# Summing the first two key/value chunks inside TensorE, and moving the first score ahead of the other query turns

## The chip, the cores and the metric

The kernel runs on one core of a Trainium2 chip. The metric is device time in microseconds (us) of one execution. Before the change it was 1057.65 us (median of 3 runs, 1057.03 to 1057.91).

A ratio below is the mean time of one kernel's fast runs over that of the kernel before in the same rounds on the same chip, so it is not quite the ratio of the medians quoted beside it.

## The reference, cut to what matters

```python
kv_pool = kv.reshape(B, H//4, 4, W//4, 4, C).mean(axis=(2, 4))   # B=4, H=384, W=32, C=128
k = v = kv_pool.reshape(B, -1, C) @ w_sr                         # 768 keys = 6 chunks of 128
a = softmax(q @ k.T / sqrt(C))                                   # 12288 queries in each batch
x = a @ v
out = (relu(x @ w_gate) * (x @ w_val)) @ w_out                   # d_ff = 1536
```

Each of the 768 keys of a batch is a mean over 4 lines (`dh`) by 4 columns (`dw`) of the key/value image, projected by `w_sr`. Nothing can be scored before a chunk of 128 keys is pooled, turned (transposed), projected and written.

## The kernel before

Batch 0 has an opening of its own, in which nothing else is there to do. The key/value image comes in three pairs of chunks, each pair in four transfers, one for each line:

```python
def kv_load(b, pair):
    parts = work.tile([128, r, 2, r, C], FP32, tag="kv_in", bufs=3)
    ...
    for dh in range(r):
        nc.sync.dma_start(parts[:, dh]..., rows[dh])       # 512 KB each
    for h in range(2):
        kv_in[b, 2 * pair + h] = parts[:, :, h]
```

VectorE adds the four lines in three instructions of 128x512; TensorE adds the four columns, as four turns that accumulate in one PSUM bank:

```python
def add_lines(eng, b, jc, i):     # i=0: lines 0+1, i=1: lines 2+3, i=2: the two sums
    ...
def turn_pooled(b, jc, pooled):
    tp = bank([128, 128])
    for i in range(n):            # n = 4 columns
        nc.tensor.matmul(tp, pooled[:, i, :], ident, is_transpose=True,
                         start=(i == 0), stop=(i == n - 1))
    kv_Ts[b, jc] = work.tile([128, 128], FP32, tag="kvT", name="kvT")
    nc.vector.tensor_copy(kv_Ts[b, jc], tp)
def project(b, jc): ...           # TensorE: w_sr times the turned chunk
def keep_keys(b, jc): ...         # VectorE: PSUM to kv16, the key write
```

The opening, cut:

```python
keep_warm(34); q_cast(0); q_turn_pe(0); keep_warm(34)      # idle matmuls
...
add_lines(nc.vector, 0, 0, 0); add_lines(nc.vector, 0, 1, 0)
add_lines(nc.vector, 0, 0, 1); add_lines(nc.vector, 0, 0, 2)
turn_pooled(0, 0, ...); add_lines(nc.vector, 0, 1, 1)
project(0, 0); keep_keys(0, 0)
for i in range(1, GRP):
    q_turn_pe(i)
    if i == 1: add_lines(nc.vector, 0, 1, 2)
for jc in range(NJC):
    scores(0, jc); turn_values(0, jc, nc.scalar.copy)
    turn_pooled(0, jc + 1, ...)
    for k in range(1, GRP): scores(k, jc)
    project(0, jc + 1)
    ...                                                     # adds of the chunks after
    keep_keys(0, jc + 1)
    ...                                                     # more adds; value products; weight loads
```

`scores` is a TensorE matmul of 128x512 and an exponential on ScalarE, for four query tiles `k`. After the six chunks the first FFN projection starts (`value_proj`), and from there TensorE is full to the end.

The softmax here doesn't subtract the row's maximum and nothing guards it: scores larger than these inputs give would overflow.

Of the kernel before, what the change touches and what calls it, by code (L numbers as in the profile page):

```python
# [9 lines left out]
FP32 = mybir.dt.float32  # L10
FP16 = mybir.dt.float16
# [5 lines left out]
def kernel(  # L17
# [22 lines left out]
    nc = tc.nc  # L40

    B, N, C = q.shape
    _, H, W, _ = kv.shape
    r = 4
    J = (H // r) * (W // r)
    NJC = J // 128
    HC = H // NJC
    D_FF = moe_w_gate.shape[1]
    NFB = D_FF // 128
    T = 512  # L50
    NS = T // 128
    NST = N // T
    NT = B * NST
    GRP = 4
# [8 lines left out]
    work = ctx.enter_context(tc.tile_pool(name="work", bufs=2))  # L63
    psum = ctx.enter_context(tc.tile_pool(name="psum", bufs=8, space=bass.MemoryType.PSUM))

    def bank(shape, dtype=FP32):
        return psum.tile(shape, dtype, tag="bank", name="bank_ps")


    q16s, qTs, q32s = {}, {}, {}  # L70

    def q_load(g):
        if not 0 <= g < NG:
            return
        b, n0 = divmod(g * GRP * T, N)
        q16 = work.tile([128, GRP * NS, C], FP16, tag="q16", bufs=2)
        nc.gpsimd.dma_start(  # L77
            q16, q[b, n0 : n0 + GRP * T, :].rearrange("(p s) c -> p s c", p=128)
        )
        q16s[g] = q16  # L80

    def q_turn(g):
        if not 0 <= g < NG:
            return
        q16 = q16s.pop(g)
        qT = work.tile([128, GRP * NS, 128], FP16, tag="qT", bufs=3)
        nc.sync.dma_start_transpose(qT, q16.rearrange("p s c -> p (s c)"))
        qTs[g] = qT
# [7 lines left out]
            q32s[i] = q32[:, i - i0]  # L96

    def q_cast(i):
        q16 = work.tile([128, NS, C], FP16, tag="q16s", bufs=2, name="q16s")
        nc.scalar.copy(q16, q32s[i])  # L100
        q16s[0, i] = q16

    def q_turn_pe(i):
        q16 = q16s.pop((0, i))
        qt_ps = bank([128, NS, 128], FP16)
        for s in range(NS):
            nc.tensor.transpose(qt_ps[:, s, :], q16[:, s, :], ident16)
        if i == 0:
            qTs[0] = work.tile([128, GRP * NS, 128], FP16, tag="qT", bufs=3, name="qT")
        nc.vector.tensor_copy(qTs[0][:, i * NS : (i + 1) * NS, :], qt_ps)  # L110

    def qT_of(k):
        s0 = (k % GRP) * NS
        return qTs[k // GRP][:, s0 : s0 + NS, :].rearrange("c s p -> c (s p)")
# [4 lines left out]
    kv_in = {}  # L119
# [11 lines left out]
    s2s, s1s, kv_Ts, key_banks = {}, {}, {}, {}  # L131

    def add_lines(eng, b, jc, i):
        if i == 0:
            s2s[b, jc] = work.tile([128, 2, r, C], FP32, tag="kv_s2", bufs=2, name="kv_s2")
        parts, s2 = kv_in[b, jc], s2s[b, jc]
        if i < 2:
            eng.tensor_tensor(s2[:, i], parts[:, 2 * i], parts[:, 2 * i + 1], op=ALU.add)  # L138
        else:
            s1s[b, jc] = work.tile([128, r, C], FP32, tag="kv_s1", bufs=2, name="kv_s1")  # L140
            eng.tensor_tensor(s1s[b, jc], s2[:, 0], s2[:, 1], op=ALU.add)  # L141
            del kv_in[b, jc], s2s[b, jc]
# [8 lines left out]
    def turn_pooled(b, jc, pooled):  # L151
        tp = bank([128, 128])
        n = pooled.shape[1]
        for i in range(n):
            nc.tensor.matmul(  # L155
                tp, pooled[:, i, :], ident, is_transpose=True,
                start=(i == 0), stop=(i == n - 1),
            )
        kv_Ts[b, jc] = work.tile([128, 128], FP32, tag="kvT", name="kvT")
        nc.vector.tensor_copy(kv_Ts[b, jc], tp)  # L160

    def project(b, jc):
        key_banks[b, jc] = bank([128, 128])
        nc.tensor.matmul(key_banks[b, jc], w_sr_f32, kv_Ts.pop((b, jc)), start=True, stop=True)  # L164

    def keep_keys(b, jc):
        nc.vector.tensor_scalar(  # L167
            kv16[:, b, jc, 0:C], key_banks.pop((b, jc)), 1.0 / (r * r), None, op0=ALU.mult
        )

    def turn_values(b, jc, copy):
        vt = bank([128, 128], FP16)
        nc.tensor.transpose(vt, kv16[:, b, jc, 0:C], ident16)  # L173
        copy(kv16[:, b, jc, C : 2 * C], vt)
# [5 lines left out]
    def scores(k, jc):  # L180
        if jc == 0:
            aTs[k] = work.tile([128, NJC, T], FP16, tag="aT", bufs=4, name="aT")
        s_ps = bank([128, T])
        nc.tensor.matmul(s_ps, kv16[:, k // NST, jc, 0:C], qT_of(k), start=True, stop=True)  # L184
        nc.scalar.activation(aTs[k][:, jc, :], s_ps, AF.Exp, scale=qk_scale)  # L185

    def values(k, jc, half):
        if jc == 0:
            x_banks[k, half] = bank([128, 2, C + 1])
            if half == 0:  # L190
                x16s[k] = work.tile([128, NS, C], FP16, tag="x16", bufs=3, name="x16")
                rinvs[k] = work.tile([128, NS], FP32, tag="rinv", bufs=3, name="rinv")
        x_ps = x_banks[k, half]
        for i in range(2):
            s = 2 * half + i
            nc.tensor.matmul(  # L196
                x_ps[:, i, :], aTs[k][:, jc, s * 128 : (s + 1) * 128],
                kv16[:, k // NST, jc, C : 2 * C + 1],
                start=(jc == 0 and i == 0), stop=(jc == NJC - 1), skip_group_check=True,
            )  # L200
# [80 lines left out]
    ident = const.tile([128, 128], FP32)  # L281
    make_identity(nc, ident)
    ident16 = const.tile([128, 128], FP16)
# [11 lines left out]
    wg16 = const.tile([128, D_FF], FP16)  # L295
    wv16 = const.tile([128, D_FF], FP16)
    wo16 = const.tile([128, NFB, 128], FP16)

    def pool_of(jc):
        return nc.gpsimd if jc == NJC - 2 else nc.vector  # L300


    idle = bank([128, 128])

    def keep_warm(n):
        for _ in range(n):
            nc.tensor.matmul(idle, ident16, ident16, start=True, stop=True)

    keep_warm(34)
    q_cast(0)  # L310
    q_turn_pe(0)
    keep_warm(34)
    for i in range(1, GRP):
        q_cast(i)
    add_lines(nc.vector, 0, 0, 0)
    add_lines(nc.vector, 0, 1, 0)
    add_lines(nc.vector, 0, 0, 1)
    add_lines(nc.vector, 0, 0, 2)
    turn_pooled(0, 0, s1s.pop((0, 0)))
    add_lines(nc.vector, 0, 1, 1)  # L320
    project(0, 0)
    keep_keys(0, 0)
    for i in range(1, GRP):
        q_turn_pe(i)
        if i == 1:
            add_lines(nc.vector, 0, 1, 2)
    for jc in range(NJC):
        scores(0, jc)
        turn_values(0, jc, nc.scalar.copy)
        ahead = jc + 1 < NJC  # L330
        if ahead:
            turn_pooled(0, jc + 1, s1s.pop((0, jc + 1)))
        for k in range(1, GRP):
            scores(k, jc)
        if ahead:
            project(0, jc + 1)
        if ahead and jc % 2 == 1:
            add_lines(nc.vector, 0, jc + 2, 1)
        if ahead:
            keep_keys(0, jc + 1)  # L340
        if jc % 2 == 1 and ahead:
            add_lines(nc.vector, 0, jc + 2, 2)
        elif jc + 3 < NJC:
            add_lines(pool_of(jc + 2), 0, jc + 2, 0)
            add_lines(nc.vector, 0, jc + 3, 0)
            add_lines(nc.vector, 0, jc + 2, 1)
            add_lines(nc.vector, 0, jc + 2, 2)
        if jc > 0:
            for k in range(2):
                for half in range(2):  # L350
                    values(k, jc - 1, half)
        if jc == 2:
            for own in (slice(0, D_FF // 2), slice(D_FF // 2, D_FF)):
                nc.gpsimd.dma_start(wv16[:, own], moe_w_val[:, own])
                nc.gpsimd.dma_start(wg16[:, own], moe_w_gate[:, own])
            q_load(1)
            q_turn(1)
            nc.gpsimd.dma_start(wo16, moe_w_out.rearrange("(fb f) c -> f fb c", f=128))
            q_load(2)
    for half in range(2):  # L360
        values(0, NJC - 1, half)
        keep_values(0, half)
# [12 lines left out]
    for k in range(LAG, last + 1):  # L375
# [4 lines left out]
        b = k // NST + 1  # L380
        at = k % NST - (NST - NJC - 6)
        for step in range(NFB):
            kO, kF = k - LAG - 1, k - LAG
            half, i = divmod(step // 2, NJC // 2)
# [4 lines left out]
            if k == LAG:  # L389
                own, left = left[:2], left[2:]  # L390
# [69 lines left out]
```

## Time and profile before

| what | value | how to read it |
|---|---|---|
| time | 1057.65 us | median of 3 runs |
| span in the profile | 1055.9 us | first to last instruction |
| first FFN projection | 38.05 us | the end of the opening |
| from there to the end | 1017.9 us | TensorE full |
| key writes of chunks 0 to 5 start at | 14.71, 18.92, 24.72, 27.30, 31.27, 33.84 us | the pace of the opening |
| clock at half | to 4.40, 11.23 to 18.05 and 21.47 to 24.88 us | the trace's clock records; before the first one, the matmul spacing |

The opening is 3.6% of the time.

### The profile page before, as it was taken

How to read it: one execution, taken by the hardware profiler on the slowest of the kernel's cores; microseconds unless marked ns; L12 is line 12 of the kernel's file. 1: busy time of each engine (PE TensorE's matmuls, PEld its weight loads, DVE VectorE, ACT ScalarE, POOL GpSimd, SP SyncE). 2: the span in 40 equal slices, each digit the busy share in tenths (PEclk: the TensorE clock that was granted, in tenths of full speed). 3: DMA queues.
4: the chain of work that ended last, by engine and by line, in shares of the span. 5: the costliest groups of instructions: out<-in, count | busy, mean ns of one | idle time of the engine just before them, and what ended most of it. 6: DMA issues, size and time to landing. Idle time of an engine off the chain costs nothing.

```text
span 1055.9 us, 26244 instructions
## 1 busy us (share of the span) xinstructions
PE 1035.0 (98%) x9998; PEld 691.4 (65%) x9998; DVE 926.2 (88%) x1809; ACT 912.2 (86%) x1758; POOL 107.1 (10%) x127
## 2 busy tenths in 40 slices
PE   6999999999999999999999999999999999999997
PEld 4566666666666666666666666666666666666664
DVE  4788889999898989898989898999888888888896
ACT  3898888888888888888888888888888888888886
POOL 2000044200000005500000003340000000000000
PEclk8999999999999999999999999999999999999999
DMA  8732365431322435523224144542331322212111
GB/s 292 125 81 52 66 195 160 72 71 46 71 67 51 86 114 144 149 66 72 56 61 86 32 86 130 149 132 56 77 79 37 82 55 64 54 45 53 46 32 46
DMA packets 125710, 90.76 MB, mean 86 GB/s; under 512 B 103312, under 2 KB 103952, under 8 KB 125584
## 3 DMA queue, kind: packets, MB, share of 16 engines
q1 hardware_dynamic: 120144, 75.85, 26.9%
q0 software_dynamic: 5440, 13.24, 7.6%
q8 instruction: 78, 1.28, 0.5%
q14 instruction: 48, 0.39, 0.1%
HBM read 52.76 MB, written 25.17 MB: 74 GB/s over the span
## 4 chain that ended last, share of the span: by engine, by line
PE 96%; DVE 1%; ACT 1%; DMA 1%; issue 0%; SPq 0%; ACTq 0%; DVEq 0%
PE bank_ps L254 24%; PE bank_ps L240 24%; PE bank_ps L229 23%; PE bank_ps L196 12%; PE bank_ps L184 12%; DMA parts<-in_kv_dram 1%; PE bank_ps L155 1%; PE bank_ps L164 1%; DVE hT L243 0%; ACT aT L185 0%; DVE kv_s L138 0%; DVE kv_s L141 0%; SPq L127 0%; ACT o_sb L264 0%; PE bank_ps L173 0%
## 5 line engine op out<-in xcount | busy, mean ns | idle before, releaser
L243 DVE SCALAR_TENSOR_TENSOR hT<-bank_ps,val 128x512 f16<-128x512 f32 x1152 | 764.2, 686 | 99.7 <-ACT val L233 70.6
L233 ACT CAST val<-bank_ps 128x512 f16<-128x512 f32 x1152 | 677.7, 590 | 118.7 <-PE bank_ps L229 115.8
L254 PEld LDWEIGHTS <-hT 128*128 128x128 f16 x4608 | 351.1, 98 | 207.2 <-issue 3.0
L254 PE MATMUL bank_ps<-wo,hT 128*128 128x128 f16 x4608 | 443.4, 219 | 2.1 <-DVE hT L243 2.0
L240 PE MATMUL bank_ps<-xT,wg 128*128 128x512 f16 x1152 | 435.7, 378 | 1.6 <-DVE hT L243 1.5
L229 PE MATMUL bank_ps<-xT,wv 128*128 128x512 f16 x1152 | 436.6, 379 | 0.4 <-ACT x L205 0.4
L185 ACT ACTIVATE aT<-bank_ps 128x512 f16<-128x512 f32 x576 | 345.8, 604 | 7.6 <-PE bank_ps L184 7.6
L196 PE MATMUL bank_ps<-kv,aT 128*128 128x129 f16 x2304 | 223.6, 220 | 0.0
L196 PEld LDWEIGHTS <-aT 128*128 128x128 f16 x2304 | 177.5, 98 | 67.9 <-issue 0.4
L184 PE MATMUL bank_ps<-qT,kv 128*128 128x512 f16 x576 | 217.7, 381 | 0.5 <-DVE kv L167 0.4
L240 PEld LDWEIGHTS <-wg 128*128 128x128 f16 x1152 | 111.5, 97 | 65.4
L229 PEld LDWEIGHTS <-wv 128*128 128x128 f16 x1152 | 112.7, 98 | 0.6 <-issue 0.5
L205 DVE CAST x<-bank_ps 128x256 f16<-128x256 f32 x186 | 76.9, 414 | 2.1 <-PE bank_ps L196 2.1
L77 POOL DMA_DIRECT2D q<-in_q_dram x23 | 12.5, 543 | 552.6 <-DMA qT<-q 552.4
L138 POOL TENSOR_TENSOR kv_s<-parts 128x512 f32<-128x512 f32 x37 | 46.5, 1269 | 167.7 <-DMA parts<-in_kv_dram 145.0
L266 DVE TENSOR_TENSOR o_sb<-bank_ps,inv 128x512 f32<-128x512 f32 x93 | 63.2, 680 | 0.0
L184 PEld LDWEIGHTS <-kv 128*128 128x128 f16 x576 | 56.6, 98 | 2.3 <-issue 0.8
L206 DVE RECIPROCAL rinv<-bank_ps 128x2 f32<-128x2 f32 x192 | 30.5, 159 | 1.0 <-ACT x L205 0.7
L141 POOL TENSOR_TENSOR kv_s<-kv_s 128x512 f32<-128x512 f32 x18 | 22.8, 1268 | 1.4
L210 DVE TENSOR_TENSOR inv<-rinv 128x4 f32<-128x4 f32 x96 | 19.7, 205 | 3.3
L155 PE MATMUL bank_ps<-ident,kv_s 128*128 128x128 f32 x24 | 5.2, 353 | 8.7 <-DVE kv_s L141 8.4
L146 POOL TENSOR_TENSOR s<-kv_s 128x256 f32<-128x256 f32 x18 | 13.1, 726 | 1.4
(39 smaller groups left out, 108.6 us busy)
## 6 DMA issues: line engine op xcount, KB each, us to landing
parts<-in_kv_dram SPq DMA_DIRECT2D x48, 512.0 KB, 6.4
out_dram<-o_sb SPq DMA_DIRECT2D x96, 256.0 KB, 2.2
q<-in_q_dram POOLq DMA_DIRECT2D x23, 512.0 KB, 5.1
xT<-x SPq DMA_TRANSPOSE x94, 2.5
q<-in_q_dram SPq DMA_DIRECT2D x1, 768.0 KB, 8.3
wv<-in_moe_w_val_dram POOLq DMA_DIRECT2D x2, 192.0 KB, 4.6
wg<-in_moe_w_gate_dram POOLq DMA_DIRECT2D x2, 192.0 KB, 5.0
wo<-in_moe_w_out_dram POOLq DMA_DIRECT2D x1, 384.0 KB, 10.0
```

What stands on the lines that cost most here:

```text
L138: eng.tensor_tensor(s2[:, i], parts[:, 2 * i], parts[:, 2 * i + 1], op=ALU.add)
L184: nc.tensor.matmul(s_ps, kv16[:, k // NST, jc, 0:C], qT_of(k), start=True, stop=True)
L185: nc.scalar.activation(aTs[k][:, jc, :], s_ps, AF.Exp, scale=qk_scale)
L196: nc.tensor.matmul(x_ps[:, i, :], aTs[k][:, jc, s * 128 : (s + 1) * 128], kv16[:, k // NST, jc, C : 2 * C + 1], start=(jc == 0 and i == 0) ...
L205: copy(x16s[k][:, own, :], x_ps[:, :, 0:C])
L206: nc.vector.reciprocal(rinvs[k][:, own], x_ps[:, :, C])
L229: nc.tensor.matmul(va_ps, wv16[:, fb * 128 : (fb + 1) * 128], xTs[k], start=True, stop=True)
L233: nc.scalar.copy(val, va_ps)
L240: nc.tensor.matmul(g_ps, wg16[:, fb * 128 : (fb + 1) * 128], xTs[k], start=True, stop=True)
L243: nc.vector.scalar_tensor_tensor(hTs[k][:, fb, :], g_ps, 0.0, vals.pop((k, fb)), op0=ALU.max, op1=ALU.mult)
L254: nc.tensor.matmul(o_ps[:, s, :], hTs[k][:, fb, s * 128 : (s + 1) * 128], wo16[:, fb, :], start=(fb == 0 and s == 0), stop=(fb == NFB - 1) ...
L266: nc.vector.tensor_tensor(o_sb, o_ps, inv2.to_broadcast([128, NS, 128]), op=ALU.mult)
```

## The change

Its intent: VectorE's six adds for chunks 0 and 1 go; instead TensorE turns each of the four lines as it lands, sixteen accumulating turns for a chunk. The first score no longer waits for the query turns of the other tiles, the cast of queries and the turned chunk get a third buffer, and the adds of later chunks move to other places.

```diff
-        q16 = work.tile([128, NS, C], FP16, tag="q16s", bufs=2, name="q16s")
+        q16 = work.tile([128, NS, C], FP16, tag="q16s", bufs=3, name="q16s")
...
+    def turn_lines(b, pair):
+        tps = [bank([128, 128]) for _ in range(2)]
+        for dh in range(r):
+            for h in range(2):
+                for dw in range(r):
+                    nc.tensor.matmul(
+                        tps[h], kv_in[b, 2 * pair + h][:, dh, dw, :], ident, is_transpose=True,
+                        start=(dh == dw == 0), stop=(dh == dw == r - 1),
+                    )
...
-    keep_warm(34)
     for i in range(1, GRP):
         q_cast(i)
-    add_lines(nc.vector, 0, 0, 0)
...
-    project(0, 0)
-    keep_keys(0, 0)
+    turn_lines(0, 0)
+    for jc in range(2):
+        project(0, jc)
+        keep_keys(0, jc)
+    add_lines(nc.vector, 0, 2, 0)
+    for jc in range(2):
+        scores(0, jc)
+        turn_values(0, jc, nc.scalar.copy)
     for i in range(1, GRP):
         q_turn_pe(i)
...
+    add_lines(nc.gpsimd, 0, 4, 0)        # then the weight loads, earlier in the program than before
...
+        if jc == 2:
+            add_lines(nc.vector, 0, 5, 0)
+            add_lines(nc.vector, 0, 4, 1)
...
         if ahead:
             keep_keys(0, jc + 1)
```

More of the change, by code (lines that the diff above doesn't have):

```diff
@@ L158, in turn_pooled, with keep_turned @@
             )
-        kv_Ts[b, jc] = work.tile([128, 128], FP32, tag="kvT", name="kvT")
+        keep_turned(b, jc, tp)
+    def turn_lines(b, pair):
[7 more added lines that the diff above has]
+                    )
+        for h in range(2):
+            del kv_in[b, 2 * pair + h]
+            keep_turned(b, 2 * pair + h, tps[h])
+    def keep_turned(b, jc, tp):
+        kv_Ts[b, jc] = work.tile([128, 128], FP32, tag="kvT", bufs=3, name="kvT")
         nc.vector.tensor_copy(kv_Ts[b, jc], tp)
@@ L297, with attend @@
     wo16 = const.tile([128, NFB, 128], FP16)
-    def pool_of(jc):
-        return nc.gpsimd if jc == NJC - 2 else nc.vector
     idle = bank([128, 128])
-    def keep_warm(n):
-        for _ in range(n):
-            nc.tensor.matmul(idle, ident16, ident16, start=True, stop=True)
-    keep_warm(34)
+    for _ in range(34):
+        nc.tensor.matmul(idle, ident16, ident16, start=True, stop=True)
+    def attend(jc, tiles=(0, 1)):
+        for k in tiles:
+            for half in range(2):
+                values(k, jc, half)
     q_cast(0)
     q_turn_pe(0)
-    keep_warm(34)
     for i in range(1, GRP):
         q_cast(i)
-    add_lines(nc.vector, 0, 0, 0)
-    add_lines(nc.vector, 0, 1, 0)
-    add_lines(nc.vector, 0, 0, 1)
-    add_lines(nc.vector, 0, 0, 2)
-    turn_pooled(0, 0, s1s.pop((0, 0)))
-    add_lines(nc.vector, 0, 1, 1)
-    project(0, 0)
-    keep_keys(0, 0)
+    turn_lines(0, 0)
[6 more added lines that the diff above has]
+        turn_values(0, jc, nc.scalar.copy)
     for i in range(1, GRP):
         q_turn_pe(i)
-        if i == 1:
-            add_lines(nc.vector, 0, 1, 2)
-    for jc in range(NJC):
+    for jc in range(2):
+        for k in range(1, GRP):
+            scores(k, jc)
+    attend(0)
+    add_lines(nc.vector, 0, 3, 0)
+    add_lines(nc.vector, 0, 2, 1)
+    add_lines(nc.vector, 0, 2, 2)
+    turn_pooled(0, 2, s1s.pop((0, 2)))
+    attend(1, [0])
+    add_lines(nc.vector, 0, 3, 1)
+    project(0, 2)
+    add_lines(nc.vector, 0, 3, 2)
+    keep_keys(0, 2)
+    add_lines(nc.gpsimd, 0, 4, 0)
+    for own in (slice(0, D_FF // 2), slice(D_FF // 2, D_FF)):
+        nc.gpsimd.dma_start(wv16[:, own], moe_w_val[:, own])
+        nc.gpsimd.dma_start(wg16[:, own], moe_w_gate[:, own])
+    q_load(1)
+    q_turn(1)
+    nc.gpsimd.dma_start(wo16, moe_w_out.rearrange("(fb f) c -> f fb c", f=128))
+    q_load(2)
+    for jc in range(2, NJC):
         scores(0, jc)
@@ L336 @@
             project(0, jc + 1)
-        if ahead and jc % 2 == 1:
-            add_lines(nc.vector, 0, jc + 2, 1)
+        if jc == 2:
+            add_lines(nc.vector, 0, 5, 0)
+            add_lines(nc.vector, 0, 4, 1)
+        if jc == 3:
+            add_lines(nc.vector, 0, 5, 1)
         if ahead:
             keep_keys(0, jc + 1)
-        if jc % 2 == 1 and ahead:
+        if jc in (2, 3):
             add_lines(nc.vector, 0, jc + 2, 2)
-        elif jc + 3 < NJC:
-            add_lines(pool_of(jc + 2), 0, jc + 2, 0)
-            add_lines(nc.vector, 0, jc + 3, 0)
-            add_lines(nc.vector, 0, jc + 2, 1)
-            add_lines(nc.vector, 0, jc + 2, 2)
-        if jc > 0:
-            for k in range(2):
-                for half in range(2):
-                    values(k, jc - 1, half)
-        if jc == 2:
-            for own in (slice(0, D_FF // 2), slice(D_FF // 2, D_FF)):
-                nc.gpsimd.dma_start(wv16[:, own], moe_w_val[:, own])
-                nc.gpsimd.dma_start(wg16[:, own], moe_w_gate[:, own])
-            q_load(1)
-            q_turn(1)
-            nc.gpsimd.dma_start(wo16, moe_w_out.rearrange("(fb f) c -> f fb c", f=128))
-            q_load(2)
+        attend(jc - 1, (0, 1) if jc > 2 else [1])
     for half in range(2):
```

## The prediction

> **What bounds the kernel now.** I read the page first, then the busy time by stretch, then the chain of waits and the timeline of the first 40 us.
>
> The page of before, engine totals and two of the rows by slice:
> ```profile
> PE 1035.0 (98%) x9998; PEld 691.4 (65%) x9998; DVE 926.2 (88%) x1809; ACT 912.2 (86%) x1758; POOL 107.1 (10%) x127
> ...
> PE   6999999999999999999999999999999999999997
> ...
> PEclk8999999999999999999999999999999999999999
> ```
> Only the first slice (26 us) and the last are not full, and in the first alone the TensorE clock is visibly held back. The windows view of before, the opening and the rest (stretch, its length, then busy us of each engine):
> ```profile
> 5.00:11.00 6.00, 2.34 (x39) 2.12 (x38) 1.81 (x4) 0.62 (x1) 0.00 (x0) 1.00 1.01 390
> 11.00:18.00 7.00, 4.90 (x25) 3.64 (x26) 4.35 (x10) 2.51 (x5) 0.00 (x0) 0.52 1.02 412
> 18.00:21.70 3.70, 1.33 (x7) 0.59 (x5) 2.93 (x6) 2.22 (x5) 0.00 (x0) 0.96 0.99 395
> 21.70:24.60 2.90, 2.71 (x11) 1.98 (x12) 0.93 (x3) 1.16 (x3) 2.77 (x4) 0.50 0.11 25
> 24.60:38.05 13.45, 10.77 (x101) 7.34 (x100) 7.24 (x20) 9.78 (x23) 2.83 (x5) 0.99 1.17 176
> ...
> 38.00:1055.90 1017.90, 1009.65 (x9786) 672.60 (x9786) 908.98 (x1769) 894.51 (x1721) 100.43 (x111) 1.00 0.33 80
> ```
> From 38 us, where the first FFN projection starts, to about 1041 TensorE stands still for only some 2 us in all. The diff touches nothing after that point, so the change can be worth no more than what it takes out of the first 38 us. That opening is a chain, not an engine's throughput. The chain of waits, its first part (start, length, what):
> ```profile
> 3.63 7.18 DMA parts<-in_kv_dram
> ...
> 10.91 0.70 DVE kv_s L138
> ...
> 11.63 0.70 DVE kv_s L141
> ...
> 12.38 1.13 PE bank_ps L155 x4
> ...
> 13.87 0.80 PE bank_ps L164 x2
> ...
> 16.47 0.43 PE bank_ps L184
> ```
> From the landing of the first pair's last line (10.81) to the first score (16.26) 5.45 us pass: two VectorE adds, four turns, a copy, a projection, a key write, and then the other query turns that stand before the score. The timeline of VectorE shows what spaces the later chunks: adds between the key writes (L167).
> ```profile
> 19.13 1.88 DVE L138 TENSOR_TENSOR kv_s<-parts 128x512 f32<-128x512 f32 x3
> 21.05 0.69 DVE L141 TENSOR_TENSOR kv_s<-kv_s 128x512 f32<-128x512 f32 x1
> ...
> 24.72 0.29 DVE L167 TENSOR_SCALAR kv<-bank_ps 128x128 f16<-128x128 f32 x1 [0.82 <-PE bank_ps L164]
> ...
> 33.84 0.29 DVE L167 TENSOR_SCALAR kv<-bank_ps 128x128 f16<-128x128 f32 x1 [0.58 <-PE bank_ps L164]
> ```
> The six key writes start at 14.71, 18.92, 24.72, 27.30, 31.27 and 33.84. The last line of all lands at 22.97, so between it and the last key write lie 10.9 us that are work and not transfer.
>
> **What the Trainium skill says.** "TensorE: Matmul & The Clock Gate", Part 1, says that a busy window of about 3.4 us lifts the clock to full and an idle one halves it. The trace agrees in outline: TensorE stops at 7.97, the clock falls at about 11.4, and score matmuls then start 0.43 us apart instead of 0.22. But the clock also falls at 21.7 after an idle of only 2.2 us, so little use suffices. The same page, Part 4, says that transposes do not count as busy for the gate. This trace does not decide that: the window before the rise at 18.0 holds transposes and score matmuls mixed. "PSUM — Partial Sum Buffer" (The four PSUM rules) says that two groups open at once in one bank clear each other's bits. The sixteen-turn groups use two banks, so this does no harm; before already accumulates four FP32 turns. "GPSIMD Engine Reference", section 1, says that GpSimd's memory interface contends with VectorE instructions that have two SBUF inputs. In before no such pair overlaps (GpSimd's add ran 21.83 to 23.10, VectorE's next add began at 23.22); the changed order may overlap them.
>
> **The change, part by part.**
>
> *Chunks 0 and 1.* Removed: six VectorE adds (6 x 0.68 = 4.1 us busy), eight turns, and 34 warming matmuls (5.91 to 7.97). Added: 32 FP32 turns. Turns start 0.11 us apart at full clock and 0.21 at half (L155 at 25.90 and 12.65). Eight turns per line are then 0.86 or 1.69 us. The lines land at 6.83, 8.21, 9.57 and 10.81, so at full clock TensorE keeps up and only the last eight lie after the landing: 10.87 + 8 x 0.107 + 0.17 tail = 11.9. Copy of the second chunk 0.3 beside the first projection, projection 0.4, key write 0.3: first score at about 12.7. The exponential, though, sits on ScalarE behind three query casts whose data lands at 12.71; with a third buffer they run 12.73, 13.26, 13.79 without the wait that held the third to 15.19. First exponential: 14.3, against 16.93 before. At half clock the turns end at 13.4 and the exponential comes at about 15.1.
>
> *Chunk 2.* VectorE's order is now: add of chunk 2 (lines 0 and 1), the three query copies, then three more adds. The first add needs the line that lands at 15.34, so it runs at 15.4, the query copies at 16.05 to 17.3 (0.44 apart), the adds 17.3, 17.9 (its line landed at 17.90) and 18.55, done at 19.25. This does not depend on the clock case above. Turns 19.4 to 20.05, copy to 20.35, two adds for chunk 3 to 21.6, key write 21.6. Before: 24.72. ScalarE finishes the eight exponentials of chunks 0 and 1 (0.49 apart, the six of the other tiles from 16.95) at about 20, so it is free.
>
> *Chunks 3 to 5.* Per chunk: score to turn 0.5, four turns 0.65, copy 0.3, one or two adds 0.6 each, key write 0.3, then the last add of the next chunk 0.65 beside the score. Key writes at about 24.4 (two adds), 26.9 and 29.5. Before: 27.30, 31.27, 33.84. GpSimd's add for chunk 4 starts at 20.5 after its line lands and is off the path (needed at 24.6). ScalarE needs 2.3 us per chunk (four at 0.49 and a copy of 0.3), so its last exponential starts at 32.1, against 36.22 before.
>
> *The sum.* Last key write 33.84 - 29.5 = 4.3; last exponential 36.22 - 32.1 = 4.1. The tail to the first FFN projection (38.05) is unchanged. So 4.1 us out of the opening, and TensorE full after it. I take off 0.4 for a fall of the clock at about 18, as little use of TensorE before that invites it (four turns would cost 0.45 more), and for contention of the GpSimd add. Gain 3.7: 1057.65 - 3.7 = 1054.0.
>
> *The moved weight loads.* Their issue on GpSimd moves from 23.05 to about 21.8, after most of the lines. The second half of the gate weights landed at 30.90; 1.2 earlier is ahead of a projection at 34. The next queries' turned copy landed at 40.33 and is first used at 46.05; both move ahead, so no new wait is due.
>
> **Rivals.**
> - *The clock rival*: if transposes leave the gate idle, the clock halves at 8.0 or 11.4 and stays there into the chunk 2 turns. For it: the skill's sentence, and 34 warming matmuls gone. Against: the query copies stand behind a landing anyway, which swallows the first microsecond. Turns of two or three chunks cost 0.45 each more: gain 2 to 3, 1055.2.
> - *The transfer rival*: everything waits for the landings, so an early first score is worthless. For it: DMA stands at 1.0 of its engines until 21.7. Against: the last line lands 10.9 us before the last key write; at about 2.6 us a chunk, the path after it is VectorE's. If chunk 4's landing (22.97) were what spaced the rest, gain 2.5: 1055.1.
> - *ScalarE takes the bound*: 24 exponentials and six copies are some 13.6 us. From 14.3 that could end at 28, so it is not the limit before 32. It would be only if chunks bunched; then the gain stays at 4 or so.
> - *A bank or order stall*: the early value groups take four of eight PSUM banks before chunk 2's turns. Each release comes from an exponential that ends before 19.4, but a slip here would hold TensorE: 1 to 2 us lost, 1055.5. If all of it goes wrong the time is still near 1057, as the opening cannot grow far.
> - *More gain*: VectorE waits at 13 to 15.4 for a landing; no rival beats 6 us, as the last landing plus two chunks and a tail sets 31 or so for the first projection: 1051.
>
> **Range and chances.** The three fast runs of before spread 0.9 us. The rivals span 1051 to 1057, the centre is 1054.0, so 1052.0 to 1056.2. Two per cent is 21 us, more than half the opening; nothing in the diff can earn it and only a gross stall could lose it: 0.01, 0.98, 0.01.
>
> **What would show it.** First exponential at 14.3 (15.1 if the clock falls); last of 32 turns starting near 11.7 with 0.11 spacing; key writes of chunks 2 to 5 at 21.6, 24.4, 26.9 and 29.5; first FFN projection at about 34.2; TensorE full from there on, in the same 1017 us. I am wrong if the turns at 0.21 spacing lag the lines, if chunk 2's keys come later than 23, if the first FFN projection waits for weights, or if time won in the opening comes back as waits in the steady part.

## The result, and the profile after

The changed kernel took 1053.73 us (median of 4 runs, 1052.34 to 1055.16), against 1057.78 in the same rounds: ratio 0.9962, 95% interval 0.9945 to 0.998. The prediction of 1054.0 (1052.0 to 1056.2), "within 2%", was right. What follows asks which of its reasons were.

The page of the kernel after, engine totals and two rows by slice:

```profile
PE 1035.5 (98%) x9988; PEld 690.8 (66%) x9988; DVE 922.1 (88%) x1803; ACT 911.8 (87%) x1758; POOL 107.2 (10%) x127
...
PE   7999999999999999999999999999999999999997
...
PEclk9999999999999999999999999999999999999999
```

VectorE lost 4.1 us of work and TensorE gained half a microsecond, in a span 4.1 us shorter. The first slice of the clock went from 8 tenths to 9. The windows view of the kernel after, cut where its clock changes (stretch, length, busy us of PE, PEld, DVE, ACT and POOL, then the granted clock, the DMA share and GB/s):

```profile
5.00:11.00 6.00, 4.02 (x34) 2.96 (x32) 0.42 (x1) 0.62 (x1) 0.00 (x0) 1.00 0.99 380
11.00:18.00 7.00, 5.30 (x34) 2.94 (x35) 3.45 (x9) 4.05 (x10) 0.00 (x0) 1.00 1.02 416
18.00:22.00 4.00, 1.97 (x19) 1.43 (x17) 3.05 (x6) 1.96 (x4) 0.20 (x1) 1.00 0.95 376
22.00:25.50 3.50, 3.33 (x14) 2.27 (x15) 1.62 (x5) 2.05 (x5) 3.50 (x6) 0.51 0.37 55
25.50:34.84 9.34, 8.16 (x78) 5.33 (x75) 4.75 (x15) 7.42 (x18) 1.89 (x3) 1.00 1.21 179
34.84:1051.80 1016.96, 1009.42 (x9786) 672.57 (x9786) 908.76 (x1769) 894.19 (x1721) 100.48 (x111) 1.00 0.34 80
```

From 11 to 18 us the clock is full where it stood at 0.52 before; after its first rise one half-clock stretch is left, from 22.04 to 25.46. (Up to 4.98 us the clock is at half too: idle matmuls start 0.107 us apart before that and 0.056 after. The view has no record there and prints 1.00.) The last row says where the gain is: the opening ends at 34.84 instead of 38.05, which is 3.21 us, and the rest takes 1016.96 us against 1017.9. Over the fourteen traces the rest took 1016.1 to 1018.3 us whichever kernel it was, so a microsecond or two of any single comparison of times is chance there. The start of the first FFN projection is the sharper measure of what the change touches.

The chain of waits of the kernel after, its opening (start, length, what):

```profile
6.97 11.00 DMA parts<-in_kv_dram
...
18.07 0.70 DVE kv_s L138
...
18.80 0.70 DVE kv_s L141
...
19.63 0.64 PE bank_ps L155 x4
...
23.74 1.28 PE bank_ps L200 x3
...
34.84 0.38 PE bank_ps L245
```

The first pair of chunks has gone from the chain altogether. It now runs on transfers until 17.98, when the last line of the second pair lands; before, it ran on transfers only to 10.81. The score matmuls in it (three in 1.28 us, 0.43 each) are those of the half-clock stretch.

The timeline of VectorE after: chunk 2's last line, and the key writes (now L183).

```profile
18.07 0.69 DVE L138 TENSOR_TENSOR kv_s<-parts 128x512 f32<-128x512 f32 x1 [0.36 <-DMA parts<-in_kv_dram]
...
21.83 0.28 DVE L183 TENSOR_SCALAR kv<-bank_ps 128x128 f16<-128x128 f32 x1
...
25.48 0.29 DVE L183 TENSOR_SCALAR kv<-bank_ps 128x128 f16<-128x128 f32 x1 [0.21 <-PE bank_ps L180]
...
28.05 0.29 DVE L183 TENSOR_SCALAR kv<-bank_ps 128x128 f16<-128x128 f32 x1
...
30.63 0.29 DVE L183 TENSOR_SCALAR kv<-bank_ps 128x128 f16<-128x128 f32 x1 [0.58 <-PE bank_ps L180]
```

The add at 18.07 is marked as released by the transfer. From it to chunk 2's key write are 3.8 us. The steps after that are 3.65, 2.57 and 2.58 us; before they were 2.58, 3.97 and 2.57. So two things show: the long step from chunk 3 to chunk 4 is gone, and another long step, inside the half-clock stretch, has come.

### The profile page after: what moved, and what is told of

It reads as the page before. It is cut to its first block, busy times and chain, and to the rows that moved or that the text cites. A ratio compares the mean times of both kernels' runs of the same rounds, so it can differ in the third digit from the quotient of the medians.

```text
span 1051.8 us, 26213 instructions
## 1 busy us (share of the span) xinstructions
PE 1035.5 (98%) x9988; PEld 690.8 (66%) x9988; DVE 922.1 (88%) x1803; ACT 911.8 (87%) x1758; POOL 107.2 (10%) x127
## 3 DMA queue, kind: packets, MB, share of 16 engines
q8 instruction: 78, 1.28, 0.5%
## 4 chain that ended last, share of the span: by engine, by line
PE 96%; DMA 2%; DVE 1%; ACT 1%; issue 0%; SPq 0%; ACTq 0%; DVEq 0%
PE bank_ps L270 24%; PE bank_ps L256 24%; PE bank_ps L245 24%; PE bank_ps L212 12%; PE bank_ps L200 12%; DMA parts<-in_kv_dram 2%; PE bank_ps L155 0%; PE bank_ps L180 0%; ACT aT L201 0%; DVE hT L259 0%; DVE kv_s L141 0%; ACT o_sb L280 0%; DVE kv_s L138 0%; PE bank_ps L189 0%; DVE x L221 0%
## 5 line engine op out<-in xcount | busy, mean ns | idle before, releaser
L176 DVE COPY kvT<-bank_ps 128x128 f32<-128x128 f32 x24 | 6.8, 284 | 9.4 <-PE bank_ps L166 5.1
```

## The experiments

Theory: the turns earn their part mostly by keeping TensorE at full clock while lines land, the moved adds remove the long step, and the early first score is worth nothing. Main rival: VectorE's six adds and the new order are the gain. Twelve kernels ran, in three batches of four, 5 timed rounds each; every result was correct. In the table, "FFN" is the start of the first FFN projection, and it and the clock are read from one trace of each kernel.

| run | median us (range) | ratio to before (95%) | FFN, us | clock at half in the opening, us |
|---|---|---|---|---|
| before | 1057.65 | 1 | 38.05 | to 4.4, 11.2 to 18.1, 21.5 to 24.9 |
| after (first result) | 1053.73 (1052.34 to 1055.16) | 0.9962 (0.9945 to 0.998) | 34.84 | to 5.0, 22.0 to 25.5 |
| after_again | 1052.86 (1052.34 to 1053.91) | 0.9957 (0.9945 to 0.997) | 33.87 | to 11.1 |
| after_warm | 1053.33 (1052.14 to 1054.32) | 0.9962 (0.9949 to 0.9975) | 34.02 | to 10.6 |
| before_warm | 1054.93 (1054.26 to 1055.99) | 0.998 (0.9966 to 0.9993) | 36.37 | to 6.3 |
| after_vectorpool | 1055.51 (1054.05 to 1056.59) | 0.9982 (0.9969 to 0.9996) | 36.37 | to 7.2, 17.4 to 20.8 |
| before_turns | 1054.57 (1054.45 to 1055.2) | 0.997 (0.9956 to 0.9984) | 35.77 | to 5.6, 19.2 to 22.6 |
| after_copies_first | 1054.33 (1053.52 to 1054.77) | 0.9964 (0.9951 to 0.9976) | 34.43 | to 4.8, 21.9 to 25.3 |
| after_pair1_turned | 1052.97 (1052.3 to 1055.4) | 0.9956 (0.9943 to 0.9968) | 33.59 | to 10.4 |
| after_all_turned | 1052.15 (1051.8 to 1052.46) | 0.9944 (0.9932 to 0.9957) | 33.09 | to 4.5 |
| after_queries_first | 1054.04 (1052.78 to 1057.37) | 0.9965 (0.9952 to 0.9979) | 34.60 | to 4.7, 21.7 to 25.2 |
| before_moved_adds | 1057.17 (1056.28 to 1058.55) | 0.9995 (0.9982 to 1.0008) | 36.22 | to 6.7, 13.6 to 17.0, 20.4 to 23.8 |
| after_vectorpool_warm | 1054.87 (1054.54 to 1055.44) | 0.9971 (0.9959 to 0.9983) | 36.38 | to 4.5 |
| after_mixed | 1050.62 (1049.77 to 1052.08) | 0.9933 (0.9921 to 0.9945) | 32.63 | to 6.1 |

The medians of the kernel before in the three batches were 1057.82, 1057.99 and 1057.58 us.

That the clock differs is no accident of single traces. Every timed run has its mean granted clock (half-clock time before the first rise is not counted in it): 0.9941 on average over the 29 runs of the kernel before in the three batches, 0.9978 over the nine of the changed kernel. By an estimate from these two means, some 8 us less at half clock in each run. Of the 29, the one with the highest clock (0.997) was the fastest, 1055.69 us.

### after_again: the changed kernel, unaltered

> The changed kernel once more, unaltered, to see how far its time and its clock move from run to run. Both theories: near 1053.7 us, ratio 0.996 to the kernel before. If the half-clock stretch (22.0 to 25.3 us in its first trace) comes at another place or not at all, the span should move with it by about 1 us.

In this trace the clock, once full, never fell before the end, and the opening ended at 33.87, 0.97 us earlier than in the first. Windows and VectorE's timeline of this run, and TensorE's with the 32 turns of the first pair:

```profile
22.00:25.50 3.50, 2.56 (x17) 1.51 (x17) 2.42 (x6) 2.50 (x6) 3.50 (x6) 1.00 0.34 48
```

```profile
24.52 0.28 DVE L183 TENSOR_SCALAR kv<-bank_ps 128x128 f16<-128x128 f32 x1
```

```profile
7.19 5.61 PE L166 MATMUL bank_ps<-ident,parts 128*128 128x128 f32 x32 [0.64 <-DMA parts<-in_kv_dram]
```

Chunk 3's key write comes 2.67 us after chunk 2's (21.85), not 3.65. So the half-clock stretch costs this kernel 0.97 us when it comes, and whether it comes differs from run to run.

Why it does can be read from the clock records. In every one of the fourteen traces they lie whole steps of 3.41 us apart, so each trace has a grid, and the grids lie differently over the same work. The grid step before the fall, in the first trace, and the two steps over the same work in this one:

```profile
18.63:22.04 3.41, 1.34 (x11) 0.99 (x10) 2.53 (x6) 1.33 (x3) 0.24 (x1) 1.00 0.92 364
...
17.95:21.36 3.41, 2.04 (x20) 1.43 (x17) 2.40 (x5) 2.03 (x5) 0.03 (x1) 1.00 1.03 407
21.36:24.77 3.41, 2.11 (x15) 1.40 (x15) 2.43 (x7) 2.16 (x5) 3.41 (x5) 1.00 0.24 56
```

TensorE was busy for 1.34 us of the step that ended in a fall, and for 2.04 and 2.11 of those that did not. Of the 111 full-clock steps in the fourteen openings, all eight with 1.38 us or less ended in a fall. Of the 103 with 1.68 or more one did (1.90, in after_vectorpool). So, as far as these traces show, where the grid falls decides whether this stretch comes.

The same trace shows something else. Its clock was at half up to 11.12 us, while the lines of the first pair landed: its turns start 0.213 us apart until then and 0.109 after. The last turn ended at 12.80 instead of 12.07 and the first score came at 13.62 instead of 12.90, and nothing came of it: first exponential 14.45 (14.42), chunk 2's key write 21.85 (21.83). A full clock while those lines land was thus worth nothing in this trace (nor in after_warm, at half up to 10.59); what counts is the clock after about 11 us, where the turns had raised it. The span itself differed by only 0.7, as the rest was a little longer here.

### after_warm: idle matmuls in three gaps

```diff
     for i in range(1, GRP):
         q_turn_pe(i)
+    fill(24)                  # idle FP16 matmuls
...
     attend(0)
+    fill(16)
...
     project(0, 2)
+    fill(16)
```

> The changed kernel with 24, 16 and 16 idle FP16 matmuls in three gaps of TensorE (after the query turns, after the first value group, after chunk 2's projection), to keep the clock full. Clock theory: no half-clock stretch, chunk 3's key write at about 24.5 instead of 25.48, about 1.0 us faster than the changed kernel (1052.7). Rival (VectorE's order is all that counts): same as the changed kernel within 0.3 us.

From its first rise at 10.59 the trace kept the full clock, chunk 3's key write came at 24.67, and the opening ended at 34.02. That is 0.8 us earlier than in the first trace, near the expected 1, but no gain on after_again, which had no stretch to lose either, and the times (1053.33 against 1052.86) show none. The size of the stretch's cost is confirmed by the trace; that idle matmuls help on average is not.

### before_warm: the kernel before at full clock

```diff
-    keep_warm(34)
+    keep_warm(112)
...
+        if jc == 1:
+            (32 idle matmuls)
         if ahead:
             turn_pooled(0, jc + 1, s1s.pop((0, jc + 1)))
```

> The kernel before with its second warming stretch lengthened from 34 to 112 matmuls and 32 more ahead of chunk 2's turns, so that the clock stays full; its pooling and order are untouched. Clock theory (half or more of the gain is that the turns keep TensorE at full clock while lines land): key write of chunk 2 at about 22.3 instead of 24.72, time about 1055.3. Rival (the gain is VectorE's six adds and the order): at most 0.6 us gained, 1057.2.

Chunk 2's key write came at 22.29 and the time was 1054.93: the clock theory's numbers, and outside what the rival allowed. Windows of this run, the stretches that stood at 0.52 and 0.50 before:

```profile
11.00:18.00 7.00, 5.48 (x61) 4.04 (x58) 4.42 (x12) 3.34 (x7) 0.00 (x0) 1.00 1.02 411
...
21.70:24.60 2.90, 1.92 (x19) 1.42 (x18) 2.18 (x3) 2.12 (x5) 2.90 (x4) 1.00 0.09 32
```

Nothing but idle matmuls was added, no add and no order was touched, and the opening got 1.68 us shorter. It would have been more: the key write of chunk 2 is 2.43 earlier, but then an add of VectorE took 1.42 us instead of 0.68 because GpSimd's add ran beside it (see after_vectorpool_warm). The rounds agree: ratio 0.998 (0.9966 to 0.9993).

### before_turns: the sixteen turns alone

```diff
-    keep_warm(34)
...
-    (VectorE's pooling of chunks 0 and 1, turn_pooled)
+    turn_lines(0, 0)
     project(0, 0)
     keep_keys(0, 0)
```

> The kernel before with one part of the change alone: chunks 0 and 1 turned line by line in TensorE (the second warming stretch gives way to the turns), everything else in the old order, query turns ahead of the first score, two cast buffers. My theory now (the turns carry the gain, through the clock and through VectorE, and the new order adds little): key write of chunk 2 at 21.2, first FFN projection at 34.2 at full clock, time 1053.4, as fast as the whole change. Rival (the order earns its part): first FFN projection a microsecond or more later than in the whole change (33.9 to 34.8), 1054.5 or more.

The opening ended at 35.77: 2.28 us gained by the turns alone, 1054.57 us. My expectation that this would be the whole change was wrong by a microsecond and a half. Three reasons are in the trace. The first is a half-clock stretch from 19.2 to 22.6, which I had left out. The second is a VectorE add that ran while GpSimd's add did (20.68 to 21.94) and took 1.55 us instead of 0.68, on the chain of waits:

```profile
20.94 1.55 DVE L138 TENSOR_TENSOR kv_s<-parts 128x512 f32<-128x512 f32 x1
```

The third is the step from chunk 3's key write (25.01) to chunk 4's (28.99), still 3.98 us. That step is the order's part, as the rival said; the other two are accidents of this trace, so the 2.28 us are rather too little for the turns.

### before_moved_adds: the moved adds alone

```diff
+        if jc == 2:
+            add_lines(pool_of(jc + 2), 0, jc + 2, 0)
+            add_lines(nc.vector, 0, jc + 3, 0)
+            add_lines(nc.vector, 0, jc + 2, 1)
         if ahead:
             keep_keys(0, jc + 1)
```

> The kernel before with one part of the new order alone: two adds of chunks 4 and 5 moved ahead of chunk 3's key write. My theory (the old place of those adds makes the step from chunk 3's keys to chunk 4's 3.97 us instead of 2.57): key write of chunk 3 0.6 later (27.9), of chunk 4 0.8 earlier (30.5), first FFN projection near 37.2, about 0.8 us gained. Rival (the place of these adds does not matter): first FFN projection at 38.0.

VectorE's timeline of this run:

```profile
25.66 1.28 DVE L138 TENSOR_TENSOR kv_s<-parts 128x512 f32<-128x512 f32 x2
26.86 0.28 DVE L167 TENSOR_SCALAR kv<-bank_ps 128x128 f16<-128x128 f32 x1
...
29.43 0.29 DVE L167 TENSOR_SCALAR kv<-bank_ps 128x128 f16<-128x128 f32 x1
```

The two adds now fill VectorE's wait for the projection; the step to chunk 3 grows by 0.53 us (23.75 to 26.86 against 2.58 before) and the step to chunk 4 shrinks by 1.40 (2.57 against 3.97): net 0.87. The opening ended 1.83 earlier, but 0.97 of that is already there at chunk 2's key write (23.75 against 24.72) and stems from this run's shorter half-clock time, 6.8 us against 10.2. The timed rounds (0.9995, interval 0.9982 to 1.0008) do not resolve 0.87 us; the trace does.

### after_queries_first: the early first score undone

```diff
-        tag="q16s", bufs=3
+        tag="q16s", bufs=2
...
+    for i in range(1, GRP):
+        q_turn_pe(i)
     add_lines(nc.vector, 0, 2, 0)
     for jc in range(2):
         scores(0, jc)
         turn_values(0, jc, nc.scalar.copy)
-    for i in range(1, GRP):
-        q_turn_pe(i)
```

> The changed kernel with its second part undone: the other query turns stand ahead of the first score again, with two cast buffers instead of three. My theory (chunk 2's keys wait for a landing at 18 us, whatever the first score does): first exponential at about 15.3 instead of 14.4, key write of chunk 2 at 21.8, time as the changed kernel within 0.4 us (1053 to 1054). Rival (the early first score is worth its 0.9 us): 0.9 us slower.

The first exponential came at 15.13 instead of 14.42, and the opening ended at 34.60, no later than the first trace of the whole change (34.84), with the same half-clock stretch in both. In the trace the early score is worth nothing; the rounds (0.9965 against 0.9962 and 0.9957, each to within 0.002) could not show 0.9 us by themselves. This edit also puts the query copies ahead of chunk 2's first add, which the next run tests alone. Chunk 2's key write tells why: 21.59, and the line it needs landed at 17.74, a distance of 3.85 us. In the kernel after it is 21.83 and 17.98 (3.85), in after_again 21.85 and 17.99 (3.86).

### after_copies_first: the query copies ahead of chunk 2's first add

```diff
-    add_lines(nc.vector, 0, 2, 0)
     ...
     for i in range(1, GRP):
         q_turn_pe(i)
+    add_lines(nc.vector, 0, 2, 0)
```

> The changed kernel with the query copies ahead of chunk 2's first add in VectorE's order. My theory (chunk 2's keys wait for the line that lands near 17.98, so the second microsecond of query copies does not matter): the exponentials of the other tiles start near 15.5 instead of 16.9, key write of chunk 2 still at 21.8, time unchanged within 0.4 us. Rival (the copies behind a landing cost what they wait, about 1.4 us): 1.4 us faster than the changed kernel.

Key write of chunk 2 at 21.44, landing at 17.59: 3.85 us once more. The opening ended at 34.43, earlier by just what the line landed earlier. Nothing was gained, as the theory said. After the change a transfer holds chunk 2, and what VectorE does before 17.98 does not matter.

### after_vectorpool and after_vectorpool_warm: VectorE's pooling in the new order

```diff
-    turn_lines(0, 0)
-    for jc in range(2):
-        project(0, jc)
-        keep_keys(0, jc)
+    (112 idle matmuls; the six adds, two turn_pooled, project and keep_keys as before)
```

> The changed kernel's order, but chunks 0 and 1 pooled by VectorE as before, with 112 warming matmuls in place of the turns so that the clock stays full. Clock theory: pooling in TensorE itself is worth little once the clock is full, about 0.7 us slower than the changed kernel (1054.4). Rival (the turns themselves are the gain): about 3 us slower, 1056.7.

The time (1055.51) lay between the two theories, and the clock had fallen from 17.4 to 20.8 all the same, so the run could not separate them. The second try adds idle matmuls in the later gaps:

```diff
+    fill(18)
     turn_pooled(0, 1, s1s.pop((0, 1)))
+    fill(8)
...
+    fill(12), fill(10), fill(14)     # after the query turns, the first value group, chunk 2's projection
```

> Once more VectorE's pooling of chunks 0 and 1 in the new order, with idle matmuls in all of TensorE's gaps, since the clock fell at 17.4 in the first try. My theory (with the clock full, the turns themselves earn about 1.1 us): no half-clock stretch before 30 us, first FFN projection at 35.0 against 33.9 in the changed kernel at full clock. Rival (the turns are worth the clock only): 33.9.

The clock stayed full, yet the opening ended at 36.38, later than either theory said. VectorE's and GpSimd's timeline of this run:

```profile
19.63 0.69 DVE L138 TENSOR_TENSOR kv_s<-parts 128x512 f32<-128x512 f32 x1 [0.23 <-DMA parts<-in_kv_dram]
...
22.25 1.63 POOL L138 TENSOR_TENSOR kv_s<-parts 128x512 f32<-128x512 f32 x1 [20.48 <-DVE kvT L176]
22.79 1.64 DVE L141 TENSOR_TENSOR kv_s<-kv_s 128x512 f32<-128x512 f32 x1
```

Against after_again chunk 2's key write is 2.50 us later (24.35 against 21.85), and two entries account for it. The line of chunk 2 landed at 19.53 instead of 17.99 (1.54). And VectorE's add of 0.69 us took 1.64 while GpSimd's add ran beside it, which itself took 1.63 instead of 1.27 (0.95). Nothing is left over for the six adds as such. So in this order the turns have no shown worth beyond the clock, and beyond doing it without idle matmuls; a run without both accidents was not had, so this stays read off the trace and not tested. (In the rounds this kernel was some 2 us slower than the changed one, 1054.87 against 1052.86.)

Why the line landed later: in this trace the queries' transfer lands 3.4 us after the one before it instead of 1.9, and in that stretch lies one packet of the instruction queue. In the kernel after the same packet lies between 18 and 19 us, and there the step between two lines is 2.38 us (17.98 to 20.36) instead of 1.28. The DMA view of the kernel after, 17 to 21 us:

```profile
q8 instruction: 1, 0.02, 1.7%
```

1.7% of 16 engines over 4 us is 1.1 us of one engine. The kernel before has no such packet in its first 24 us and no such step; before_warm has one between 11 and 12 us, and its step is there (10.59 to 13.91). The programs with more TensorE instructions early fetch the next block earlier. But the size varies (in after_mixed, with a packet at 20.70, the step is only 0.2 us longer), and a second packet of after_vectorpool_warm, at 20.98, delays no line (landings at 20.81, 22.08 and 23.32). That the packet causes the delay is argued from coincidences and was not tested alone.

### after_pair1_turned, after_all_turned, after_mixed: going further

In after_pair1_turned the second pair is turned line by line too, the turns of a line interleaved with the scores of the first pair. In after_all_turned the third pair follows, except that GpSimd still adds two lines of chunk 4. In after_mixed VectorE adds the first two lines of chunks 2, 3 and 5, so that those have 12 turns instead of 16:

```diff
+    add_lines(nc.vector, 0, 2, 0)
+    add_lines(nc.vector, 0, 3, 0)
...
+    for h in range(2):
+        turn_four(tps[h], s2s.pop((0, 2 + h))[:, 0], True, False)
+    for dh in range(2, r):
+        for h in range(2):
+            turn_four(tps[h], kv_in[0, 2 + h][:, dh], False, dh == r - 1)
```

> The changed kernel with the second pair of chunks (2 and 3) turned line by line in TensorE as well, and VectorE left with chunks 4 and 5. My theory (after the first pair VectorE's adds space the key writes): keys of chunks 2 and 3 at 20.3 and 20.7 instead of 21.8 and 24.5 to 25.5, chunk 5's at 28.3, first FFN projection at 32.9, time about 1052.0 against 1052.9 to 1053.7 for the changed kernel. Rival (TensorE's in-order turns block the scores, or ScalarE bounds it): no gain or slower.

> All three pairs turned in TensorE; GpSimd adds two lines of chunk 4 as before, so that the weight loads keep their place. My theory: keys of chunks 4 and 5 at about 26.3 and 26.6, last exponential near 30.6, first FFN projection at 32.2, time about 1051.4. Rival (ScalarE, 24 exponentials and six copies, is the bound by now, or turns waiting for lines block the scores): no earlier than with one pair more, 1052 or slower.

> All pairs summed in TensorE, but with the first two lines of chunks 2, 3 and 5 added by VectorE, which is idle there, so that TensorE has 12 turns for them instead of 16. My theory (with all pairs turned TensorE has become the opening's bound: its chain from 14 to 33 us is TensorE almost alone): keys of chunks 2 and 3 at 19.2 and 19.7, of 4 and 5 at 25.5 and 26.0, first FFN projection at 32.3, time about 1051.3 against 1052.15. Rival (the landing near 24 us and ScalarE set it): no earlier than 33.0.

With the second pair turned, the keys of chunks 2 and 3 came at 20.01 and 20.45 as expected (against 21.83 and 25.48), but chunk 5's only at 29.38 and the projection at 33.59 instead of 32.9. Most is taken back before chunk 4's turns at 25.27: they come after VectorE's last sum for that chunk (done at 25.12) and after ScalarE's exponentials of chunks 2 and 3 (done at 25.15, and the ones on the chain of waits), so both held them. With all pairs turned, chunks 4 and 5 came at 26.25 and 26.69, as expected, but the tail was longer and the projection at 33.09, not 32.2; from 14.3 to 31.3 us its chain of waits is TensorE alone. Taking 12 turns off TensorE (four each of chunks 2, 3 and 5), with the scores of chunks 2 and 3 ahead of the last pair's turns, brought 32.63. The chain of waits of after_mixed:

```profile
16.86 2.71 PE bank_ps L346 x24
...
22.30 2.96 ACT aT L201 x6
```

TensorE's turns still lead to chunks 2 and 3, but the six exponentials of those chunks now fill the chain from 22.3 to 25.3: in that stretch ScalarE has taken over. The time was 1050.62 us, ratio 0.9933 (0.9921 to 0.9945): it beats the kernel before by 7 us and the changed kernel by 2 to 3 (1053.73 and 1052.86 in its two sets of runs), in part because this trace's rest was short (1016.17). Its first estimates (19.2 and 25.5 for the keys) were 0.9 and 0.3 us too early; the second pair's lines landed 0.3 us later than in the kernel after.

## Why the prediction was right or wrong

**What bounds it, and how much can be won: right.** TensorE is full after the opening, and the rest did not change beyond chance (1016.96 against 1017.9).

**Chunks 0 and 1: right, within 0.25 us.** The turns of a line start 0.11 us apart, each burst of eight takes 1.09 us against landings 1.3 us apart, the last ends at 12.1. First score 12.90 (predicted 12.7), first exponential 14.42 (14.3). The full-clock case of the two was the true one in this trace. In after_again and after_warm the clock was at half up to 11.12 and 10.59, and the exponential still came at 14.45 and 14.59: as the prediction says, it sits behind the query casts.

**Chunk 2: right.** Key write 21.83 (predicted 21.6). The prediction said that this does not depend on the first score, and noted that the add at 17.9 needs a line that lands at 17.90. It was in fact held by that landing (18.07 after 17.98), and in after_again, after_warm, after_copies_first and after_queries_first by the same 3.85 or 3.86 us. That "this does not depend on the clock case" was right too (21.85 in after_again). So the transfer rival, which was to leave a gain of 2.5 us, was right about this one chunk, and the working had it in already.

**Chunks 3 to 5: the steps were right, one term was mis-sized.** At full clock (after_again) the key writes came at 24.52, 27.09 and 29.66, against 24.4, 26.9 and 29.5. In the first trace they came 1.0 us later. The term is "I take off 0.4 for a fall of the clock at about 18 ... and for contention of the GpSimd add". The clock fell at 22.04, not at 18, and the stretch cost 0.97 us, because the score matmuls and the projection slow down with the turns; in another run it did not fall there at all. The contention cost VectorE nothing in the changed kernel: GpSimd's add started at 21.80 when VectorE's adds were all but done (21.91). In after_again it started at 21.34 and was itself stretched, to 1.72 us, off the chain. It did hold VectorE in four experiments, for 0.20, 0.74, 0.87 and 0.95 us.

**The sum was right partly by luck.** Predicted 3.7 us out of the opening and nothing elsewhere; the first trace shows 3.21 out of the opening and 0.9 in the rest, which moves by about that much by chance. At full clock the opening gained 4.18, against the 4.1 before the deduction.

**Where the gain comes from: not said by the prediction, and not where the change's name puts it.** The parts add up. The turns alone took 2.28 us off the opening (before_turns). The moved adds net 0.87 (by its steps, before_moved_adds). The early first score gave 0 (after_queries_first). Together 3.15, against 3.21 for the whole; each comes from one trace with its own half-clock stretches, and that of the turns from one with the lost 0.87 us, so the close agreement is partly chance. Taken at full clock (after_again), 2.87 of the 4.18 us lie before chunk 2's key write and 1.31 between it and chunk 4's. Idle matmuls alone, without touching a single add, gave 2.43 of the first; the moved adds alone gave 0.87 of the second. The 0.88 left, and what the turns are worth by themselves, are not isolated. The clock rival had the right mechanism and the wrong direction: it feared that turns would not hold the clock, and they do; in after_again they even raised it.

**The moved weight loads: wrong, without effect.** Predicted "from 23.05 to about 21.8"; they were issued at 23.01. GpSimd's add stands before them, and its line landed at 21.63 instead of 20.46, behind the step of 2.38 us described above. The second half of the gate weights landed at 30.82, still ahead of the projection at 34.84. The next queries' turned copy landed at 41.26, later than before (40.33), and is first used at 42.83 instead of 46.05: the slack fell from 5.7 to 1.6 us. No wait came of it.

**Rivals.** ScalarE as the bound: no more than before; the chain of waits of both kernels has the same 1.58 and 2.07 us of exponentials among the last chunks. A stall by banks or order: none; the first value group ran at 18.04, straight after the scores.

## What to carry to other kernels

In a start-up phase, moving a reduction into TensorE as accumulating turns can pay by keeping TensorE's clock up for the work that follows, where it would otherwise stand still; test it against plain idle matmuls before crediting the removed adds. Ask of every part of such a change whether a landing stands behind it: a part that only brings work up to the same landing earlier, as the early first score did, is free and worthless. When the effect is a few microseconds in a thousand, read it from the traces at the point where the touched phase ends, since the rest of the run moves by a microsecond by itself.

## What the Trainium skill lacked or had wrong

- "TensorE: Matmul & The Clock Gate", Part 4, says that transposes do not count as busy for the clock gate. Here the FP32 turns do: in after_again TensorE ran nothing else from 7.19 to 12.80 us and the clock rose from half to full at 11.12. In the kernel after it ran only turns (four FP16, 32 FP32) from 5.7 to 12.0 and the clock stayed full until 22.04; the kernel before, standing still from 7.97 to 12.38, lost it at 11.23.
- The same page, Part 1, asks for an idle window of about 3.4 us before the clock falls. The half-clock stretches do last 3.41 us or twice that, in agreement, but the steps before a fall were not idle: eight had TensorE busy for 0.16 to 1.38 us, and a ninth for 1.90. How much use is enough is not on the page; in these openings 1.68 us of 3.41 held the clock and 1.38 did not, with that ninth step the one exception.
- "GPSIMD Engine Reference", section 1, names the contention with VectorE instructions of two SBUF inputs, and that section gives no size. In the four traces in which an add of VectorE (two 128x512 FP32 inputs) started while GpSimd's ran, it took 0.88, 1.42, 1.55 and 1.64 us instead of 0.69, and each time ended 0.55 us after GpSimd's: it waited, and did not share.
- "Runtime: NRT & Kernel Launch", Instruction fetch mechanics, calls the cost of crossing a 16 KiB block mostly hidden. In a stretch where the transfers fill all engines (share 1.0), the traces show one such packet holding one engine for 1.0 to 1.1 us, and in eleven traces the step between landings there 0.2 to 1.5 us longer; one packet, at 20.98 us in after_vectorpool_warm (share 0.88 around it), came without a longer step, and the cause was not tested.
